# Attention scores on two 64-row halves of TensorE: three products per head, keys not doubled, queries not stacked

## The chip, the cores and the metric

The kernel runs on one core of one Trainium2 chip. The metric is the device time of one launch in microseconds (us). A core has five engines that work side by side and meet at semaphores: TensorE (matmuls; in the profile PE, its weight loads PEld), VectorE (DVE), ScalarE (ACT), GpSimd (POOL) and SyncE (SP, which here only issues DMA transfers). Matmul results go to PSUM, which is divided into banks; everything else lies in SBUF, with 128 partitions.

## What is computed

Block-causal attention, and a gated linear layer behind it:

```python
def _attn_ref(q, k, v):                       # each (8, 8, 576, 64)
    scores = np.matmul(q, k.transpose(0, 1, 3, 2)) / np.sqrt(64)
    mask = (pos[:, None] // 64) >= (pos[None, :] // 64)
    scores = np.where(mask, scores, -1e9)
    attn = softmax(scores)                    # max subtracted, + 1e-9 in the sum
    return np.matmul(attn, v)

def _moe_ref(x, w_gate, w_val, w_out):        # x is (4608, 512), d_ff 1536
    gate = 1 / (1 + np.exp(-(x @ w_gate)))
    return (gate * (x @ w_val)) @ w_out
```

The queries and keys are scaled by 5.7 and the gate's weights by 8, so the softmax and the gate are sharp. For this the kernel splits float32 operands into a high part H (float32r, which TensorE takes at its fast rate) and the rest L, and adds products of the parts. The three weights come as 64-bit floats and are converted on the chip.

## The kernel before

**Stages.** The 64 heads are worked on as 32 pairs of two heads (4 pairs per batch). One pair is one round of the loop `for p in range(n + 1)` (L753). In a round, the first half of pair p (`first`, L487: scores, exponentials) alternates with the second half of pair p-1 (`last`, L488: transposes of the probabilities, the product with V) and with `prep(p + 1)` (L244), which splits the next pair's keys and queries; the loads of pair p+2 are issued in between (L766 and L797). As soon as a batch of four pairs is done, a third of the first MLP layers (`mlp1`, L548, four of twelve blocks of d_ff) runs as filling: after each step of attention the loop takes some matmuls of it (L777 to L783). The weights of this filling are converted piece by piece during pairs 3 to 7 (`CONV_PLAN`, L25), mostly on VectorE. After the last pair comes the rest of the MLP (from L800), a seven-product scheme over two thirds of d_ff. It isn't touched, except that its buffers `raw` (L647) are named by tags of the first stage.

**The operands of the scores.** Queries and keys arrive by DMA in 32-wide blocks (L209 to L216) and are transposed on VectorE, so that the 64 features of head 0 lie in partitions 0 to 63 and those of head 1 in 64 to 127. A product of TensorE contracts over all 128 partitions, so each head is given all of them: `KD` holds, for each head, the high part of the keys twice, one copy in each half of the partitions, and likewise the rest; `QS` holds the high part of the scaled queries in one half and the rest in the other. One product with the high keys thus gives qH kH + qL kH, and a second with the rest of the keys adds qH kL + qL kL. To get there, prep casts the keys on ScalarE (L256), subtracts on VectorE (L257), and issues three copies from SBUF to SBUF for the keys (two at L260, one at L280) and four for the queries (L279), all on SP's queue. The queries are first split in place in the tiles `rk` and `rq` into which the loads of the pair after the next will go. Pair 0 has a path of its own with fewer steps (L262, L282).

**The scores.** `s_main(i)` (L330) does 128 query rows against the first 128 (i+1) keys, for i = 3, 2, 1, 0, so 512, 384, 256 or 128 columns. For i = 3 and 2 each head has its own PSUM bank, and one head's two products, the mask (a memset, L349), the maximum (a reduction, L350) and the exponential (L342) are issued before the other head's. For i = 1 and 0 both heads share one bank, one memset (L358) and one reduction (L359). `s_tail` (L365) does the last 64 query rows of both heads at once: `QS` is zero outside its own columns, so one product gives rows of head 0 and rows of head 1; that takes four products for each of two halves of the 576 keys.

**Order.** Each engine works through its own instructions in order. All matmuls of attention are recorded under the helper's line 225, all transposes under 228. The pool `ps_a` has six banks that are handed out in turn. The helper `behind` (L57) puts one instruction after another on the same engine without a semaphore; `mark("SP", ...)` in the loads (L214) makes the fetches of the MLP's weights (L77) queue behind them.

Of the kernel before, what the change touches and what calls it, by code (L numbers as in the profile page):

```python
# [29 lines left out]
def attn_glu_kernel(ctx: ExitStack, tc: tile.TileContext, q, k, v, w_gate, w_val, w_out, out):  # L30
    nc = tc.nc
# [117 lines left out]
    with ExitStack() as s2:  # L149
# [25 lines left out]

        QSs = [cv.tile([P, 2, 640], F32R, name=f"QS{i}") for i in range(2)]
        for QS in QSs:
            nc.gpsimd.memset(QS[:, 0, S:].bitcast(F32), 0.0)
            nc.gpsimd.memset(QS[:, 1, 0:64].bitcast(F32), 0.0)

# [4 lines left out]
        QM = (0, 128)  # L185
        QT = (512, 0)

        pairs = [(b, hp) for b in range(B) for hp in range(NP)]
        state = {}
# [7 lines left out]
        def load(p, what):  # L197
            b, hp = pairs[p]
            h0 = 2 * hp
            for name in what:  # L200
# [9 lines left out]
                for h in range(2):  # L210
                    parts = [(0, 0, S)] if name == "k" or h == 0 else [(64, 0, 512), (0, 512, 64)]
                    for j in range(2):
                        for c0, t0, n in parts:
                            mark("SP", nc.sync.dma_start(  # L214
                                out=r[64 * h + 32 * j:64 * h + 32 * j + 32, c0:c0 + n].rearrange("p (t a) -> p t a", a=32),
                                in_=src[b, h0 + h, t0:t0 + n, 32 * j:32 * j + 32].rearrange("(t p) a -> p t a", p=32)))  # L216
# [26 lines left out]

        def prep(p):  # L244


            KD = cv.tile([P, 2, 2, S], F32R, name="KD", bufs=2)
            QS = QSs[p % 2]
# [5 lines left out]
            if p:  # L254

                nc.scalar.copy(out=KD[:, 0, 0], in_=kT)  # L256
# [4 lines left out]
            else:  # L261
                for h in range(2):  # L262
                    s, o = halves(h)
                    nc.scalar.copy(out=KD[s, h, 0], in_=kT[s])
                    nc.vector.tensor_sub(out=KD[s, h, 1], in0=kT[s], in1=KD[s, h, 0].bitcast(F32))
                    nc.sync.dma_start(out=KD[o, h].bitcast(F32), in_=KD[s, h].bitcast(F32))
# [4 lines left out]
            if p:  # L271

                qH, qL = rk.bitcast(F32R), rq.bitcast(F32R)
                nc.scalar.mul(out=qH, in_=qT, mul=scale)
                nc.vector.scalar_tensor_tensor(out=qL, in0=qT, scalar=scale, in1=rk, op0=ALU.mult, op1=ALU.subtract)
                for e, src in enumerate((rk, rq)):
                    for h in range(2):
                        s, o = halves(h)
                        dma = nc.sync.dma_start(out=QS[o if e else s, h, 64 * h:64 * h + S].bitcast(F32), in_=src[s])  # L279
                behind(nc.sync.dma_start(out=B, in_=A).ins, dma.ins)  # L280
            else:
                for h in range(2):  # L282
                    s, o = halves(h)
                    c = slice(64 * h, 64 * h + S)
                    nc.scalar.mul(out=QS[s, h, c], in_=qT[s], mul=scale)
                    nc.vector.scalar_tensor_tensor(out=QS[o, h, c], in0=qT[s], scalar=scale,
                                                   in1=QS[s, h, c].bitcast(F32), op0=ALU.mult, op1=ALU.subtract)
# [4 lines left out]
            if whole(p):  # L292
                VS = at.tile([P, 5, 2 * D], F32, name="VS", bufs=2)
                nc.gpsimd.tensor_copy(out=VS, in_=rv)
                state[p] = KD, QS, VS
                return
# [11 lines left out]
            state[p] = KD, QS, (VS, V4)  # L308

        def attend(p):  # L310
            b, hp = pairs[p]
            KD, QS, VS = state.pop(p)
# [17 lines left out]
            def s_main(i):  # L330
# [5 lines left out]
                def scores(ps, h):  # L336
                    for e in range(2):
                        matmul(ps, lhsT=QS[:, h, QM[h] + i * P:QM[h] + (i + 1) * P], rhs=KD[:, h, e, :n],
                                         start=(e == 0), stop=(e == 1))

# [4 lines left out]
                if i >= 2:  # L345
                    for h in range(2):
                        ps = bank()[:, :n]
                        scores(ps, h)
                        nc.vector.memset(ps[0:64, n - 64:n], -1e9)  # L349
                        mark("DVE", nc.vector.tensor_reduce(out=nm[:, c0 + h:c0 + h + 1], in_=ps, axis=AX.X,  # L350
                                                            op=ALU.max, negate=True))
                        exps(ps, h)
                        yield
                else:
                    pv = bank()[:, :2 * n].rearrange("p (h n) -> p h n", h=2)
                    for h in range(2):
                        scores(pv[:, h], h)
# [3 lines left out]
                    for h in range(2):  # L361
                        exps(pv[:, h], h)
# [645 lines left out]
```

## Time and profile before

| what | value |
|---|---|
| median of 3 runs | 1294.96 us (1289.36 to 1296.46) |
| the profiled execution | 1295.23 us |
| its span, first to last instruction | 1293.1 us |
| mean granted clock of TensorE | 0.983 |
| instructions | 21797, of them 7312 matmuls |
| moved by DMA | 189.31 MB in 269359 packets |

In the profile's rows, `L225 PE MATMUL bank<-KD,QS 128*128 128x288 f32` means: line 225, engine PE, a matmul that reads the tiles KD and QS and writes a bank, on 128 rows and 128 columns of the array, with 128x288 elements streamed. Behind x stands the number of instructions, then the busy time in us and the mean duration of one in ns, then the idle time of the engine just before them and what ended it. A matmul's end is modelled and matmuls overlap, so the sum of their durations is more than the time they take. A row of the timeline gives the start, the length from the first start to the last end, and how many of a kind follow each other. A row of the chain gives a start, a length and what the end of the program waited for in that time. The row `PEclk` gives the clock granted to TensorE in tenths, in 40 slices of the span; 9 is 90% or more.

### The profile page before, as it was taken

What the parts mean: (1) busy time and instruction counts of PE and PEld (TensorE: products, weight loads), DVE (VectorE), ACT (ScalarE), POOL (GpSimd) and SP (SyncE); (2) the same over time, 40 slices, a digit from 0 to 9 for tenths busy, and PEclk for the clock granted to TensorE, in tenths of its full rate; (3) what the DMA queues carried; (4) which work ended last, traced back from release to release, by engine and by line L of the source; (5) the groups of instructions that cost most, each with busy time, mean ns of one, the idle gap of its engine ahead of it and who ended that gap; (6) DMA issues with size and microseconds to landing.
All of it is one profiled execution on the core that took longest, in us unless ns stands there. A gap on an engine that the chain in (4) does not pass through costs nothing.

```text
span 1293.1 us, 21797 instructions
## 1 busy us (share of the span) xinstructions
PE 1219.4 (94%) x7312; PEld 1129.5 (87%) x7312; DVE 996.0 (77%) x2153; ACT 736.8 (57%) x1829; POOL 390.0 (30%) x400
## 2 busy tenths in 40 slices
PE   4879899999999999999999899999999999999996
PEld 3769779999899998999989888999989989999995
DVE  6789988978889788887797897776679557656743
ACT  4767667877788787887754445344445424313411
POOL 1113223434344343443430013312321323542431
PEclk8989999999999999999999899999999999999999
DMA  7787676676766767668531424522538542552443
GB/s 146 159 199 187 161 143 151 127 178 125 157 144 129 176 127 155 155 127 189 128 108 56 166 82 159 187 80 109 187 139 297 195 154 69 170 180 67 144 148 97
DMA packets 269359, 189.31 MB, mean 146 GB/s; under 512 B 199808, under 2 KB 220288, under 8 KB 268608
## 3 DMA queue, kind: packets, MB, share of 16 engines
q1 hardware_dynamic: 259392, 169.04, 51.4%
q10 hardware_dynamic: 9856, 18.88, 4.1%
q8 instruction: 58, 0.95, 0.3%
q14 instruction: 53, 0.43, 0.1%
HBM read 94.37 MB, written 47.19 MB: 109 GB/s over the span
## 4 chain that ended last, share of the span: by engine, by line
PE 59%; DVE 17%; DMA 10%; ACT 5%; issue 4%; SPq 3%; POOL 1%; ACTq 0%; DVEq 0%; POOLq 0%
PE b L817 20%; PE bank L225 10%; PE m L875 8%; PE m L114 7%; PE m L123 5%; PE b L875 4%; PE bank L228 3%; DMA KD<-KD 2%; DMA pr<-part_d 2%; DVE P L397 2%; PE bank L114 2%; SPq L214 1%; DVE XL L716 1%; ACT P L342 1%; DVE KD L257 1%
## 5 line engine op out<-in xcount | busy, mean ns | idle before, releaser
L817 PE MATMUL b<-XH,w 128*128 128x384 f32 x1344 | 353.7, 338 | 9.7 <-ACT ost L576 3.1
L817 PEld LDWEIGHTS b<-XH,w 128*128 128x128 f32 x1344 | 246.0, 189 | 17.1 <-DVE v L853 5.1
L817 PE MATMUL b<-XL,w 128*128 128x384 f32 x672 | 225.7, 337 | 0.0
L225 PE MATMUL bank<-KD,QS 128*128 128x288 f32 (+4 forms) x768 | 162.2, 334 | 27.6 <-DMA KD<-KD 20.3
L225 PEld LDWEIGHTS bank<-KD,QS 128*128 128x128 f32 x768 | 118.7, 197 | 38.1 <-issue 18.9
L342 ACT ACTIVATE P<-bank,nm 128x512 f32<-128x512 f32 (+3 forms) x256 | 134.1, 529 | 29.2 <-DVE nm L359 16.3
L817 PEld LDWEIGHTS b<-XL,w 128*128 128x128 f32 x672 | 127.3, 190 | 1.3
L875 PE MATMUL m<-wo,hH 128*128 128x512 f32 x384 | 125.3, 392 | 0.3 <-ACT wo L684 0.3
L228 PE MATMUL bank<-ident,P 128*128 128x128 f32 x640 | 94.8, 280 | 15.7 <-DVE P L397 15.7
L114 PE MATMUL m<-XH,wv 128*128 128x288 f32 x448 | 105.0, 302 | 2.7 <-DVE h L135 1.4
L114 PE MATMUL m<-XH,wg 128*128 128x288 f32 x448 | 105.8, 303 | 0.2 <-ACT t L133 0.2
L890 POOL TENSOR_TENSOR pr<-pr,pr 128x512 f32<-128x512 f32 x36 | 48.0, 1333 | 167.4 <-DMA pr<-part_d 163.1
L228 PEld LDWEIGHTS bank<-ident,P 128*128 128x128 f32 x640 | 77.5, 144 | 22.8 <-issue 9.3
L225 PE MATMUL bank<-G1H,VS 128*128 128x320 f32 (+2 forms) x352 | 93.3, 346 | 0.9 <-ACT G1H L321 0.9
L397 DVE TENSOR_SCALAR P<-P,sm 128x512 f32<-128x512 f32 (+3 forms) x256 | 90.8, 412 | 1.2
L840 ACT ACTIVATE g<-g 128x384 f32<-128x384 f32 x72 | 37.0, 524 | 94.3 <-DVE g L853 64.5
L875 PEld LDWEIGHTS m<-wo,hH 128*128 128x128 f32 x384 | 72.0, 188 | 14.3 <-ACT wo L684 0.6
L715 ACT CAST XH<-XB 128x1536 fp32r<-128x1536 f32 (+2 forms) x72 | 65.8, 938 | 29.3 <-DVE XB L713 22.0
L323 DVE TENSOR_TENSOR G1L<-bank,G1H 128x512 fp32r<-128x512 f32 (+1 forms) x120 | 74.3, 626 | 10.5 <-ACT G1H L321 9.1
L321 ACT CAST G1H<-bank 128x512 fp32r<-128x512 f32 (+1 forms) x120 | 63.6, 545 | 31.3 <-PE bank L228 27.8
L114 PEld LDWEIGHTS m<-XH,wv 128*128 128x128 f32 x448 | 76.2, 189 | 3.4 <-DVE h L135 1.9
L716 DVE TENSOR_TENSOR XL<-XB,XH 128x1536 fp32r<-128x1536 f32 (+2 forms) x72 | 77.3, 1081 | 1.5 <-ACT XH L715 1.5
(178 smaller groups left out, 2936.2 us busy)
## 6 DMA issues: line engine op xcount, KB each, us to landing
KD<-KD SPq DMA_DIRECT2D x95, 288.0 KB, 3.9
pr<-part_d SPq DMA_DIRECT2D x72, 256.0 KB, 3.6
QS<-rqk SPq DMA_DIRECT2D x124, 144.0 KB, 3.1
rqk<-in_k_dram SPq DMA_DIRECT2D x128, 72.0 KB, 3.3
xT_d<-xT ACTq DMA_DIRECT2D x32, 288.0 KB, 3.1
XB<-xT_d SPq DMA_DIRECT2D x16, 576.0 KB, 5.7
part_d<-ost SPq DMA_DIRECT2D x36, 256.0 KB, 3.9
out_dram<-ost SPq DMA_DIRECT2D x36, 256.0 KB, 2.8
```

What stands on the lines that cost most here:

```text
L114: mm = nc.tensor.matmul(ps, lhsT=lh, rhs=rh, start=(i == 0), stop=(i == n - 1))
L123: mm = nc.tensor.matmul(ps, lhsT=lh[:, f, t * P:(t + 1) * P], rhs=rh, start=(i == 0), stop=(i == n - 1))
L225: pe_last[:] = [nc.tensor.matmul(*args, **kw).ins]
L228: pe_last[:] = [nc.tensor.transpose(*args).ins]
L321: mark("ACT", nc.scalar.copy(out=dst[0], in_=src))
L323: mark("DVE", nc.vector.tensor_sub(out=dst[1], in0=src, in1=dst[0].bitcast(F32)))
L342: mark("ACT", nc.scalar.activation(out=Pi[:, h], in_=ps, func=AF.Exp, bias=nm[:, c0 + h:c0 + h + 1], accum_out=sm[:, c0 + h:c0 + h + 1]))
L397: mark("DVE", nc.vector.tensor_scalar_mul(Pi[:, h], Pi[:, h], sm[:, c0 + h:c0 + h + 1]))
L715: nc.scalar.copy(out=XO[j][0][:, a:b], in_=x)
L716: sub = nc.vector.tensor_sub(out=XO[j][1][:, a:b], in0=x, in1=XO[j][0][:, a:b].bitcast(F32))
L817: mm = nc.tensor.matmul(ps, lhsT=lh, rhs=rh, start=(first and k == 0), stop=(k == n - 1), skip_group_check=not first)
L875: mm = nc.tensor.matmul(po[t], lhsT=lh[:, f, t * P:(t + 1) * P], rhs=rh, start=(half == 0 and i == 0), stop=(half == 1 and i == 5))
```

## The change

The two heads' operands stay where the transposes leave them: `KQ` holds kH, kL, qH and qL, head 0 in partitions 0 to 63, head 1 in 64 to 127. Each score product works on 64 rows of the array, `tile_position=(64 * h, 0)`, and there are three per head, qH kH + qH kL + qL kH; the product of the two rests is left out. The products of the two heads alternate and write two banks. At all four widths each head now has its own bank, memset and reduction. The tail still uses all 128 rows: two small copies on GpSimd put the last 64 queries of each head into `QB`, which is zero elsewhere, and three products do both heads. The seven copies inside SBUF are gone, the load of the queries has four issues instead of six, pair 0 takes the same path as the others, the loads no longer mark SP's queue, and the buffers `raw` have tags of their own.

```diff
-        QSs = [cv.tile([P, 2, 640], F32R, name=f"QS{i}") for i in range(2)]
...
+        QBs = [at.tile([P, 2, 2, D], F32R, name=f"QB{i}") for i in range(2)]
+        for QB in QBs:
+            nc.gpsimd.memset(QB.bitcast(F32), 0.0)
...
+        PARTS = ((2, 0), (2, 1), (3, 0))
...
-                    parts = [(0, 0, S)] if name == "k" or h == 0 else [(64, 0, 512), (0, 512, 64)]
                     for j in range(2):
-                        for c0, t0, n in parts:
-                            mark("SP", nc.sync.dma_start(
...
+                        nc.sync.dma_start(
+                            out=r[64 * h + 32 * j:64 * h + 32 * j + 32].rearrange("p (t a) -> p t a", a=32),
+                            in_=src[b, h0 + h, :, 32 * j:32 * j + 32].rearrange("(t p) a -> p t a", p=32))
...
+            KQ = cv.tile([P, 4, S], F32R, name="KQ", tag="KD", bufs=2)
...
-                nc.scalar.copy(out=KD[:, 0, 0], in_=kT)
-                nc.vector.tensor_sub(out=KD[:, 0, 1], in0=kT, in1=KD[:, 0, 0].bitcast(F32))
-                A, B = (KD[s, 0].bitcast(F32) for s in (slice(0, 64), slice(64, 128)))
-                for dst in (KD[0:64, 1], KD[64:128, 1]):
-                    nc.sync.dma_start(out=dst.bitcast(F32), in_=B)
...
+            nc.scalar.copy(out=KQ[:, 0], in_=kT)
+            nc.vector.tensor_sub(out=KQ[:, 1], in0=kT, in1=KQ[:, 0].bitcast(F32))
...
-                        dma = nc.sync.dma_start(out=QS[o if e else s, h, 64 * h:64 * h + S].bitcast(F32), in_=src[s])
-                behind(nc.sync.dma_start(out=B, in_=A).ins, dma.ins)
...
+            nc.scalar.mul(out=KQ[:, 2], in_=qT, mul=scale)
+            nc.vector.scalar_tensor_tensor(out=KQ[:, 3], in0=qT, scalar=scale, in1=KQ[:, 2].bitcast(F32),
+                                           op0=ALU.mult, op1=ALU.subtract)
+            for h in range(2):
+                nc.gpsimd.tensor_copy(out=QB[rows(h), :, h], in_=KQ[rows(h), 2:4, S - D:].bitcast(F32))
...
+                pss = [bank()[:, :n] for _ in range(2)]
+                for j, (a, b_) in enumerate(PARTS):
                     for h in range(2):
...
+                        matmul(pss[h], lhsT=KQ[rows(h), a, i * P:(i + 1) * P], rhs=KQ[rows(h), b_, :n],
+                               start=(j == 0), stop=(j == 2), tile_position=(64 * h, 0))
+                for h, ps in enumerate(pss):
+                    nc.vector.memset(ps[0:64, n - 64:n], -1e9)
+                    mark("DVE", nc.vector.tensor_reduce(out=nm[:, c0 + h:c0 + h + 1], in_=ps, axis=AX.X,
+                                                        op=ALU.max, negate=True))
+                    exps(ps, h)
...
-                    for h in range(2):
-                        for e in range(2):
-                            matmul(ps, lhsT=QS[:, h, QT[h]:QT[h] + P], rhs=KD[:, h, e, 288 * half:288 * half + 288],
...
+                    for j, (a, b_) in enumerate(PARTS):
+                        matmul(ps, lhsT=QB[:, a - 2].rearrange("p h q -> p (h q)"),
+                               rhs=KQ[:, b_, 288 * half:288 * half + 288], start=(j == 0), stop=(j == 2))
...
-            return (cv.tile([P, 4 * P, 2], U32, name="raw", tag=f"QS{i}"),
+            return (cv.tile([P, 4 * P, 2], U32, name="raw", tag=f"raw{i}"),
```

More of the change, by code (lines that the diff above doesn't have):

```diff
@@ L343, in exps @@
                                                      accum_out=sm[:, c0 + h:c0 + h + 1]))
[L345 removed]
+                pss = [bank()[:, :n] for _ in range(2)]
+                for j, (a, b_) in enumerate(PARTS):
                     for h in range(2):
[L347 to L352, printed above, removed]
[L353 to L363 removed]
+                        matmul(pss[h], lhsT=KQ[rows(h), a, i * P:(i + 1) * P], rhs=KQ[rows(h), b_, :n],
[5 more added lines that the diff above has]
+                    exps(ps, h)
+                    if i >= 2 or h:
+                        yield
             def s_tail():
```

50 lines of the change are left out of this document (6 added, 44 removed).

## Prediction

> **What bounds the kernel now.** I read four views in this order: the page, the table of stretches, the timeline of TensorE, and the chain of waits. On the page three rows matter: the share of each engine, the granted clock in 40 slices, and the group of all score products.
>
> ```profile
> PE 1219.4 (94%) x7312; PEld 1129.5 (87%) x7312; DVE 996.0 (77%) x2153; ACT 736.8 (57%) x1829; POOL 390.0 (30%) x400
> PEclk8989999999999999999999899999999999999999
> L225 PE MATMUL bank<-KD,QS 128*128 128x288 f32 (+4 forms) x768 | 162.2, 334 | 27.6 <-DMA KD<-KD 20.3
> ```
>
> A share of the whole span says little, so I cut the span at the first score product of pairs 1, 4, 9 and 31, at the end of the first GLU part and at the end. Columns: us, busy time (and instructions) of PE, PEld, DVE, ACT and POOL, clock, DMA share, GB/s.
>
> ```profile
> 0.00:27.05 27.05, 8.69 (x33) 7.50 (x33) 15.70 (x34) 11.98 (x29) 3.44 (x14) 0.88 0.78 150
> 27.05:78.06 51.01, 41.81 (x227) 35.43 (x228) 38.62 (x108) 35.10 (x101) 4.25 (x4) 0.90 0.81 173
> 78.06:188.21 110.15, 97.75 (x598) 86.81 (x597) 101.20 (x246) 77.49 (x216) 28.21 (x25) 0.95 0.74 170
> 188.21:635.16 446.95, 434.89 (x3059) 410.24 (x3058) 381.53 (x929) 350.27 (x998) 169.95 (x196) 1.00 0.68 148
> 720.00:1293.10 573.10, 552.88 (x2862) 512.06 (x2860) 391.51 (x682) 218.85 (x381) 164.71 (x144) 0.99 0.43 143
> ```
>
> There are two regimes. From 188 to 635 us, pairs 9 to 30 (22 pairs), TensorE is busy 434.89 of 446.95 us at the full clock of 1.00: a microsecond of matmul more or less per pair is one on the clock. Before 188 us, pairs 0 to 8, it isn't: in pairs 1 to 3 no engine is busy throughout and the DMA share is 0.81; in pairs 4 to 8 VectorE is busy 101.20 of 110.15 us. After 635 us nothing is changed but the names of two buffers; it only moves.
>
> **What a score product costs.** Matmuls overlap in the trace, so the mean duration isn't the price; the distance between two starts is. A run of n of one shape lasts one duration and n-1 distances.
>
> ```profile
> 508.54 0.62 PE L123 MATMUL m<-wo,hH 128*128 128x512 f32 x2
> 509.00 0.39 PE L123 MATMUL m<-wo,hL 128*128 128x512 f32 x1
> ...
> 1000.63 0.51 PE L817 MATMUL b<-XH,w 128*128 128x384 f32 x2
> ...
> 1000.98 0.33 PE L817 MATMUL b<-XL,w 128*128 128x384 f32 x1
> ```
> ```profile
> 299.80 0.56 PE L225 MATMUL bank<-KD,QS 128*128 128x288 f32 x3
> 300.20 0.29 PE L114 MATMUL m<-XH,wv 128*128 128x288 f32 x1
> ...
> 305.06 0.67 PE L225 MATMUL bank<-KD,QS 128*128 128x256 f32 x4
> ```
> ```profile
> 510.46 0.64 PE L225 MATMUL bank<-KD,QS 128*128 128x128 f32 x4
> ```
> ```profile
> L225 PE MATMUL bank<-KD,QS 128*128 128x256 f32 x88 | 14.1, 283 | 0.0
> L225 PE MATMUL bank<-KD,QS 128*128 128x128 f32 x88 | 13.8, 279 | 0.0
> ```
>
> So 512 columns cost 0.62-0.39 = 0.23 us, 384 cost 0.51-0.33 = 0.18, 288 cost (0.56-0.29)/2 = 0.13, 256 cost (0.67-0.28)/3 = 0.13, 128 cost (0.64-0.28)/3 = 0.12. The last two hardly differ, because the weight load sets the distance there:
>
> ```profile
> 510.44 0.53 PEld L225 LDWEIGHTS bank<-KD,QS 128*128 128x128 f32 x4
> 510.88 0.19 PEld L123 LDWEIGHTS m<-wo,hH 128*128 128x128 f32 x1
> ```
>
> (0.53-0.19)/3 = 0.113 us per load. Now a pair (the 88 products of 256 columns in these 447 us are 4 in each of 22 pairs). Before, the main score tiles issue two products for each of two heads at 512, 384, 256 and 128 columns: 4 x (0.23+0.18+0.13+0.12) = 4 x 0.66 = 2.64 us. After, there are three products per head, each on half of the rows. Every matmul of this trace uses 128 rows, so no row shows whether two halves work at once. The ends are: one after another, 6 x 0.66 = 3.96 us (+1.32); both streams and loads in parallel, 3 x 0.66 = 1.98 (-0.66). Between them, streams in parallel but loads one at a time, as in every row above: a step of two heads then takes 0.23 at 512 and 2 x 0.113 = 0.226 at the other widths, 3 x (0.23+0.678) = 2.72 (+0.08). The tail stays on all 128 rows and goes from 8 to 6 products of 288: 2 x 0.13 = -0.26. Net per pair and over 22 pairs: +1.06 (+23), -0.92 (-20), -0.18 (-4). I take the middle one, -4: the loads in the rows come singly, and the two heads have different rows and different banks, so nothing else that the code shows ties their streams together. The Trainium skill, TensorE: Matmul & The Clock Gate, Part 3, says that matmuls in distinct row groups run concurrently, and gives 3.07x for four; by it alone the term would be -20, and no run here shows it yet.
>
> **What changing the layout costs.** The four main tiles lie between work on the full array (the MLP products, transposes and the tail), so the array goes from whole to halves and back 4 times a pair: 8 changes, 176 in 22 pairs. No row shows one. The lower end is 0: matmuls of unlike kinds follow without a gap in the rows above. The upper end is a restart: the matmuls already running finish, and the next load has nothing to hide under. A wait of TensorE shows this:
>
> ```profile
> 302.62 0.41 PE L225 MATMUL bank<-G1L,VS 128*128 128x320 f32 x1
> 302.87 0.31 PE L225 MATMUL bank<-G1H,VS 128*128 128x320 f32 x1
> 303.02 0.31 PE L225 MATMUL bank<-G1L,VS 128*128 128x320 f32 x1
> ```
>
> The uncovered load adds 0.41-0.31 = 0.10; a matmul lasts 0.31-0.15 = 0.16 beyond the distance to the next start (303.02-302.87 = 0.15). So at most 0.26. I take 0.15, a little over the middle and nearer to the restart, because by those rows a product is still under way for 0.16 us when the next could start, and it would have to be out of the way: 176 x 0.15 = +26. The Trainium skill, TensorEngine Tiling (Array Packing), Key Properties, states that switching the mode drains TensorE; it gives no price, and speaks against this change.
>
> **What the transfers were worth.** Gone are 3 copies of keys and 4 of queries per pair; loads of q and k go from 10 to 8 issues.
>
> ```profile
> KD<-KD SPq DMA_DIRECT2D x95, 288.0 KB, 3.9
> ...
> QS<-rqk SPq DMA_DIRECT2D x124, 144.0 KB, 3.1
> ```
> ```profile
> 7.83 3.36 DMA KD<-KD
> ...
> 11.33 1.20 PE bank L225 x2
> ...
> 18.59 4.25 DMA KD<-KD
> ...
> 22.92 3.88 DMA KD<-KD
> ...
> 27.05 2.04 PE bank L225 x4
> ```
> ```profile
> L269 DVE STREAM_TRANSPOSE rvT<-rqk 128x576 f32<-128x576 f32 x32 | 24.5, 767 | 0.2
> L274 ACT ACTIVATE rqk<-rvT 128x576 fp32r<-128x576 f32 x31 | 21.3, 688 | 13.1 <-DVE rvT L269 8.9 <-DVE nm L381 3.9
> L275 DVE SCALAR_TENSOR_TENSOR rqk<-rvT,rqk 128x576 fp32r<-128x576 f32 x31 | 27.1, 874 | 3.9 <-ACT rqk L274 3.8
> ```
>
> - Pair 0: its first product waits until 11.33 us for a copy. Without it the way is transpose, cast and rest of q from 7.2 us on, 0.77+0.69+0.87 = 2.3, so 9.5 at the latest: about -2.
> - Pair 1: two copies end the wait at 27.05. Without them those 2.3 us start at about 18.6, so 21: -6 at most. Pair 0's own second half then fills some of it; I take -4.
> - Pairs 1 to 3: 51.0 us with VectorE busy 38.6, so -12 at most. The copies and the loads behind them share SP's queue; the loads of pair p+2 no longer wait for copies that read rq and rk. I take -4.
> - Pairs 4 to 8: VectorE has 9.0 us free, less what is added to it. Added are, per pair, two reductions' fixed part and two memsets net.
>
> ```profile
> L350 DVE TENSOR_REDUCE nm<-bank 128x1 f32<-128x512 f32 x64 | 43.2, 681 | 0.5
> L377 DVE TENSOR_REDUCE nm<-bank 128x1 f32<-128x288 f32 x64 | 27.4, 440 | 3.9 <-PE bank L225 3.5
> L349 DVE MEMSET bank<- 64x64 f32 x128 | 14.0, 112 | 28.9 <-PE bank L225 27.4 <-ACT KD L256 0.6
> L358 DVE MEMSET bank<- 64x128 f32 x64 | 10.6, 165 | 5.3 <-PE bank L225 3.9
> ```
>
>   681 and 440 ns over 224 columns give 1.08 ns a column and 0.13 us fixed; 2 x 0.13 + 4 x 0.112 - 2 x 0.165 = +0.38 us a pair, +2 in five pairs. Freed: late weight and key copies, as the one of 5.61 us below, -5 of the 9. Net -3.
> - Pairs 9 to 30: TensorE waited for these copies 2.4 us in all: -1. VectorE's 0.38 us hides there (381.53 of 446.95 busy); if TensorE had no work left, it would cost 8.
>
> ```profile
> 160.14 5.61 DMA KD<-KD
> ```
> ```profile
> PE bank L225 <- DMA KD<-KD: 2.4, 2, 1.4
> ```
>
> Together -14; between -5 (only pairs 0 and 1, partly) and -25 (every bound reached). The two small copies per pair on POOL are on no path: POOL is busy 169.95 of 446.95, and the next pair's tail, which reads them, comes a pair later. They are queued ahead of the copy of V, which waits for TensorE anyway; without that cover each would cost about its own duration, some 0.3 us by the copy of 64x128:
>
> ```profile
> L306 POOL COPY V<-rvT 64x128 f32<-64x128 f32 x24 | 8.1, 337 | 49.1 <-DMA rvT<-in_v_dram 24.5 <-PE bank L225 8.6 <-PE m L114 7.9
> ```
>
> Dropping mark("SP") from the loads lets weight fetches pass them in SP's queue; I cost that at nothing beyond the above, since those weights are used a pair later. A score bank's first reduction now waits for five products instead of two, and two banks are held at once, not one, at 256 and 128 columns; with six banks and other matmuls between, I cost it at 0, at most about 0.5 us a pair (three products more).
>
> **The sum.** The profiled execution took 1295.2 us (1293.1 of span and 2.1 around it), 0.3 over the median of the three runs shown. 1295.2 - 14 (transfers) - 4 (products) + 26 (changes of layout) = 1303.2; I say 1303. About 0.5%, 6.5 us, is what a measurement of this kernel can tell from no change, so this stands just beyond it.
>
> **Rivals.**
> 1. Free changes. Halves and whole array follow each other as unlike matmuls do now, with no gap. Then 1295 - 14 - 4 = 1277, and with parallel loads 1261; say 1270. For it: the copies vanish, and no row has a gap between unlike matmuls. Against it: all of those use the same 128 rows. It decides once a change costs under some 0.06 us (176 x 0.06 = 11).
> 2. Full drain: at every change TensorE finishes all that runs and loads uncovered, 176 x 0.26 = +46, 1295 - 14 - 4 + 46 = 1323. For it: the restart at 302.62 shows what that costs. Against: in all other rows a load runs beside the matmul before it, and may do so across a change too. The rule in the Trainium skill, TensorEngine Tiling (Array Packing), Key Properties, would mean this case if nothing of it is hidden.
> 3. No parallel streams. The heads' products run one after another: 1295 - 14 + 23 = 1304 with free changes, 1330 with 0.15 each; say 1320. For it: every row shows one stream at a time. Against: the heads share neither rows nor banks.
> 4. The transfers were hidden anyway: pairs 1 to 8 are held by VectorE and the chain of softmax, and only pair 0 and part of pair 1 gain. -14 shrinks to -5, the rest as forecast: 1312. For it: VectorE's 101.20 of 110.15 us. Against: the copies end the waits of pairs 0, 1 and 8 in the chain.
>
> **How the numbers follow.** Forecast 0.32 (own range 1275 to 1313: a change at 0.05 to 0.2, loads parallel or single), free changes 0.29, full drain 0.17, no parallel streams 0.16, hidden transfers 0.06. Faster, under 1288.7: 0.27 of rival 1 and 0.12 of the forecast, 0.39. Within 0.5%: 0.02 of rival 1, 0.08 of the forecast, 0.02 of rival 3, 0.01 of rival 4, 0.13. Slower, over 1301.7: 0.12 of the forecast, 0.17, 0.14 and 0.05 of rivals 2, 3 and 4, 0.48. Single cases of the forecast lie on both sides, so the sign is nearly open. The range from 1267 to 1335 leaves out about 0.07 below (rival 1 with parallel loads) and 0.12 above (rivals 2 and 3 with both dear changes and one stream).
>
> **What would show each step.** Parallel streams: in the new profile two score products of 512 columns, one per head, start within a few hundredths of a microsecond of each other, and a block of six spans about 3 x 0.23 plus one duration, not 6 x 0.23. Loads: starts 0.11 us apart at 128 and 256 columns if they come singly. Layout changes: a gap before the first and after the last product of each block of six, in PEld, which no semaphore ends; 0.15 is forecast, 0 is rival 1, 0.26 is rival 2. Transfers: the first product before 10 us, pair 1 near 21 us, pair 9 near 174 instead of 188. I am wrong if the block of six has no gap at its ends, if the heads don't overlap, or if pair 9 doesn't start earlier.

## The result and the profile after

The kernel after took 1335.95 us, median of four runs (1333.62 to 1339.28), against 1295.28 of the kernel before in four runs beside it: ratio 1.0325, interval 1.0286 to 1.0364. That is 33 us above the forecast of 1303, and 1 us above the top of its range. The profiled execution took 1333.62 us, with a span of 1331.8.

Rows of the profile of after, as shown for before: engines, clock, and the score products, which here stand in two rows (the main tiles, and the tail).

```profile
PE 1281.2 (96%) x7504; PEld 1132.0 (85%) x7504; DVE 998.1 (75%) x2279; ACT 736.6 (55%) x1827; POOL 408.7 (31%) x462
PEclk9999999999999999999999999999999999999999
L220 PE MATMUL bank<-KQ 64*128 64x512 f32 (+3 forms) x768 | 145.0, 358 | 9.0 <-ACT KQ L257 9.0
L220 PE MATMUL bank<-KQ,QB 128*128 128x288 f32 x192 | 36.6, 318 | 1.6 <-ACT P L311 1.5
```

The idle time ahead of the score products fell from 27.6 to 10.6 us, the granted clock is 0.9 or more in every slice (0.992 on average, 0.983 before), and yet TensorE is busy 61.8 us longer. The stretches of after, cut as before at the first score product of pairs 1, 4, 9 and 31 and at the end of the first GLU part:

```profile
0.00:21.39 21.39, 8.48 (x38) 6.88 (x40) 13.08 (x32) 9.75 (x23) 4.43 (x16) 1.00 0.80 199
21.39:73.98 52.59, 45.93 (x247) 33.95 (x247) 41.04 (x124) 36.22 (x105) 7.10 (x10) 0.94 0.50 97
73.98:182.72 108.74, 101.35 (x632) 82.42 (x632) 104.92 (x272) 78.53 (x220) 30.97 (x35) 1.00 0.39 89
182.72:668.82 486.10, 486.10 (x3184) 419.39 (x3183) 379.35 (x1006) 348.42 (x988) 184.33 (x239) 1.00 0.30 68
668.82:758.60 89.78, 86.29 (x545) 79.05 (x545) 69.59 (x167) 46.14 (x113) 15.60 (x18) 0.98 0.31 101
758.60:1331.80 573.20, 553.02 (x2866) 510.29 (x2864) 390.07 (x682) 217.54 (x380) 166.25 (x144) 0.99 0.42 143
```

The stretch from pair 31 to the end of the first GLU part was in before:

```profile
635.16:720.00 84.84, 83.35 (x542) 77.50 (x543) 67.40 (x155) 43.06 (x106) 19.46 (x18) 1.00 0.35 112
```

Pair 9 starts 5.5 us earlier (182.72 against 188.21). Then pairs 9 to 30, the late stretch from here on, take 486.10 us instead of 446.95: +39.15, nearly the whole loss. Pair 31 with the end of the first GLU part takes 4.9 us more (89.78 against 84.84); some 1.4 us of that are six MLP products of 512 columns that ran ahead of the cut in before and run behind it in after. The last stretch is the same. In the late stretch TensorE is busy every microsecond, where before it was idle for 12 (434.89 of 446.95). So the copies' waits are gone, and the time has gone into the products or between them. Two places of the timeline of after show where; first a tile of 384 columns, engine PE and then PEld:

```profile
320.01 0.43 PE L114 MATMUL m<-XH,wv 128*128 128x288 f32 x2
320.37 0.79 PE L220 MATMUL bank<-KQ 64*128 64x384 f32 x3
321.09 0.50 PE L220 MATMUL bank<-G,VS 128*128 128x256 f32 x2
```
```profile
320.37 0.47 PEld L220 LDWEIGHTS bank<-KQ 64*128 64x128 f32 x3 [0.16 <-issue]
321.08 0.41 PEld L220 LDWEIGHTS bank<-G,VS 128*128 128x128 f32 x3 [0.25 <-ACT P L311]
```

Only three of the six products stand here; the other head's three come later, after other work. **In:** two products of 288 columns start at 320.01, 0.13 apart, so the next could start at 320.27 and starts at 320.37: a gap of 0.10. Its weights are loaded at the same moment, 320.37, not under the product before: three products 0.18 apart and one duration of 0.33 make 0.69, and the row says 0.79, so 0.10 is the uncovered load. **Out:** three distances of 0.18 end at 320.91, plus that 0.10 is 321.01; the next product starts at 321.09, 0.08 later, with its load at 321.08, uncovered again (0.50 for two of 256 columns instead of 0.28+0.13 = 0.41). So at this tile a change of layout costs a gap of 0.08 to 0.10 and a load of about 0.10: 0.17 to 0.20 us, each way.

Then a tile of 512 columns whose six products stand together:

```profile
337.94 0.28 PE L220 MATMUL bank<-G,VS 128*128 128x256 f32 x1
338.15 0.98 PE L220 MATMUL bank<-KQ 64*128 64x512 f32 x6
339.06 0.45 PE L220 MATMUL bank<-G,VS 128*128 128x256 f32 x2
```

Six products take 0.98 us, as long as three would by the distances: 2 x 0.23 + 0.39 + 0.10 of load = 0.95, while six one after another would take 1.64. The heads run side by side, if they stand together. Counted through the trace of after, they mostly don't: of 197 blocks of half-array products 136 hold three, which I take for those of one head (the rows name no head), and 55 hold six. The order in which TensorE gets its instructions is fixed when the kernel is built. I take it that it goes by when banks are expected to come free: a tile's two banks come free at different times, so three products of one head are put in, then other work, then the other three. e5 and e15 below fit this: with both banks claimed first and the order forced, the six stay together. In the late stretch there are 146 blocks instead of the 88 that I had assumed (4 tiles in 22 pairs): 292 changes instead of 176.

The trace shows the same picture at every one of these changes, in and out: the first load begins together with its product (within 3 ns), 0.07 us before the modelled end of the product ahead. Between whole-array products the next one starts 0.16 us before that end (median), so each change leaves a gap of 0.09 us. Measured block by block (up to the second product behind it, less the usual distances), the median extra is 0.31 us at 128 columns, 0.35 at 256 and 0.37 at 384: 0.16 to 0.19 per change, about 0.17 over all of them.

### The profile page after: what moved, and what is told of

Read it like the earlier page. It is cut to its first block, busy times and chain, and to the rows that moved or that the text cites. A ratio compares the mean times of both kernels' runs of the same rounds, so it can differ in the third digit from the quotient of the medians.

```text
span 1331.8 us, 21723 instructions
## 1 busy us (share of the span) xinstructions
PE 1281.2 (96%) x7504; PEld 1132.0 (85%) x7504; DVE 998.1 (75%) x2279; ACT 736.6 (55%) x1827; POOL 408.7 (31%) x462
## 4 chain that ended last, share of the span: by engine, by line
PE 76%; DVE 10%; DMA 5%; POOL 3%; issue 2%; ACT 2%; SPq 1%; POOLq 0%; ACTq 0%; DVEq 0%
PE bank L220 19%; PE b L777 17%; PE m L114 14%; PE m L835 8%; PE m L123 7%; PE bank L223 6%; PE b L835 4%; DMA pr<-part_d 3%; DVE XL L676 2%; PE bank L114 1%; POOL pr L850 1%; DMA XB<-xT_d 1%; DVE nm L322 1%; POOL hL L785 1%; DMA rqk<-in_k_dram 1%
## 5 line engine op out<-in xcount | busy, mean ns | idle before, releaser
L220 PE MATMUL bank<-KQ 64*128 64x512 f32 (+3 forms) x768 | 145.0, 358 | 9.0 <-ACT KQ L257 9.0
L220 PEld LDWEIGHTS bank<-KQ 64*128 64x128 f32 x768 | 91.1, 191 | 45.7 <-issue 20.1
L322 DVE TENSOR_REDUCE nm<-bank 128x1 f32<-128x512 f32 (+3 forms) x256 | 120.2, 480 | 3.2
L114 PE MATMUL m<-XH,wg 128*128 128x288 f32 x448 | 110.1, 310 | 0.0
L114 PE MATMUL m<-XH,wv 128*128 128x288 f32 x448 | 109.5, 308 | 0.0
L223 PEld LDWEIGHTS bank<-ident,P 128*128 128x128 f32 x640 | 74.7, 142 | 17.9 <-ACT P L311 7.1
L141 POOL TENSOR_TENSOR hL<-h,hH 128x288 fp32r<-128x288 f32 (+1 forms) x56 | 48.3, 862 | 103.1 <-ACT hH L140 85.5
```

Of the source, the lines that this page charges most:

```text
L114: mm = nc.tensor.matmul(ps, lhsT=lh, rhs=rh, start=(i == 0), stop=(i == n - 1))
L220: pe_last[:] = [nc.tensor.matmul(*args, **kw).ins]
L223: pe_last[:] = [nc.tensor.transpose(*args).ins]
```

## The experiments

**Theory:** the loss is the number of blocks of half-array products, two changes of 0.19 us each, and what a split block loses in side-by-side running. **Rivals:** products on half the rows are slow in themselves or never run side by side; or the waits moved to something else.

**e1_together and e2_together_serial.** One tile of two banks for both heads, so that both come free at once; in e2 also the order is forced, head 0's three products first.

```diff
+ pair = ps_a.tile([P, 2, 512], F32, name="pair", bufs=1)
- pss = [bank()[:, :n] for _ in range(2)]
+ pss = [pair[:, h, :n] for h in range(2)]
```

> Changed kernel, but the two heads' main scores lie in one PSUM tile of two banks (one such tile, four single banks left), so that all six products of a tile become ready at once and stay together: 246 changes of layout instead of 394, and the heads' streams always side by side. Theory (a change of layout costs about 0.19 us, and splitting the six also puts the heads one after another): -28 for the changes, about -24 for the streams, some 15 given back as waits of TensorE, 1299 (1290 to 1310). Rival 1 (half-array products are simply more products, the order doesn't matter): 1330 or more. Rival 2 (holding two banks per tile is what hurts): no faster than 1336, since here they are held even more strictly.

> As the run before, but within the six the three products of head 0 come first and then the three of head 1, in a fixed order: the same number of layout changes, the same banks, but no streams side by side except at the seam. Theory: about 1.9 us more per pair, 22 to 32 pairs bound by TensorE, less some waits: 1335 (1325 to 1345). Rival (the nearly equal starts in the trace are only records, the array works through them one after another): equal to the run before within 5 us.

Measured: 1456.38 us (ratio 1.1265, 1.1224 to 1.1306) and 1466.25 (1.1338, 1.1301 to 1.1376). Both missed. The waits of e1 from 200 to 700 us (total, times, longest) and its products:

```profile
PE pair L220 <- ACT P L311: 45.6, 39, 5.3
```
```profile
400.93 0.79 PE L220 MATMUL pair<-KQ 64*128 64x384 f32 x6 [1.00 <-ACT P L311]
404.89 0.62 PE L220 MATMUL pair<-KQ 64*128 64x256 f32 x6 [1.25 <-ACT P L311]
411.53 0.55 PE L220 MATMUL pair<-KQ 64*128 64x128 f32 x6 [0.45 <-ACT P L311]
```

There is one such tile, and each tile of scores waits until ScalarE has read the last; the granted clock of the profiled execution is 0.946, against 0.992 of after. What the runs do show is in the last rows: six products of 128 columns in 0.55 us. One duration is 0.27, so five steps take 0.28; with one load at a time, five steps of 0.113 would take 0.57. The weight loads of the two heads run side by side too. And e2's blocks are no longer than e1's:

```profile
402.77 0.80 PE L220 MATMUL pair<-KQ 64*128 64x384 f32 x6 [1.00 <-ACT P L311]
406.74 0.63 PE L220 MATMUL pair<-KQ 64*128 64x256 f32 x6 [1.25 <-ACT P L311]
413.38 0.56 PE L220 MATMUL pair<-KQ 64*128 64x128 f32 x6 [0.44 <-ACT P L311]
```

though head 1's three come behind head 0's three. The starts in e2's blocks still come in twos, 0.01 us apart. The record names no head, but in the blocks of three of after no two starts are closer than 0.11 us, so I read each two as one of each head: within a block, the order doesn't matter. Why e2 takes 10 us more than e1 stays open.

**e3_full_array.** No change of layout at all: all products on the whole array, so that both heads are summed. All else of the change stays.

```diff
- matmul(pss[h], lhsT=KQ[rows(h), a, i * P:(i + 1) * P], rhs=KQ[rows(h), b_, :n], ..., tile_position=(64 * h, 0))
+ matmul(pss[h], lhsT=KQ[:, a, i * P:(i + 1) * P], rhs=KQ[:, b_, :n], ...)
```

> Changed kernel, but each main score product uses all 128 rows without a tile position, so that it sums the scores of both heads (that part of the result is changed); same number of products, same loads, banks, VectorE and ScalarE work, no copies, no change of layout. Theory: all 394 changes at 0.19 go, -75; the products always one after another, +22; waits come back, +15: 1298 (1288 to 1310). Rival 1 (three products instead of two are the cost): 1336 or more, since nothing runs side by side any more. Rival 3 (the lost copies and the new order of loads cost): 1336.

Measured: 1298.87 (ratio 1.0056, 1.0038 to 1.0074). The half-array layout as built costs 37 us, although here all six products of a tile run one after another. Its pairs 1 to 3 and its late stretch:

```profile
23.10:69.74 46.64, 41.51 (x247) 34.99 (x247) 40.59 (x123) 35.85 (x105) 7.16 (x10) 0.99 0.51 107
179.10:633.10 454.00, 452.22 (x3186) 430.09 (x3185) 384.99 (x1007) 346.28 (x989) 183.69 (x239) 1.00 0.32 73
```

**e4_three_blocks.** As e1, and the 256- and 128-column tiles' twelve products in one block.

> As the first run of this set, but the products of the two narrow tiles (256 and 128 columns) are issued together into one pair of banks: 184 changes of layout instead of 246. Theory: 62 x 0.19 = -12 against the first run, about 1287 (1278 to 1297). Rival (the price is not per change): equal to the first run, or slower since the softmax of the narrowest tile starts earlier than it is needed.

Measured: 1408.31 (1.0901, 1.0869 to 1.0934), a miss. It is 48 us less than e1, but the wait for the one two-bank tile hides any count.

**e5_claimed.** Banks as in after, but a 64-column whole-array product writes into the second bank first, and the six follow it in order.

```diff
+ if (j, h) == (0, 0):
+     matmul(pss[1][:, :64], lhsT=KQ[:, 2, :P], rhs=KQ[:, 0, :64], start=True, stop=True)
+ before = pe_last[0]
  matmul(pss[h], ...)
+ behind(pe_last[0], before)
```

> Changed kernel with six single banks again, but ahead of the six products of each main tile stands a product of 64 columns on the full array into the second head's bank (overwritten by that head's first product), and the seven are chained in order. So the six only start when both banks are free, and stay together, without the two-bank tile that made TensorE wait in the first set. 256 changes of layout instead of 394. Theory (0.19 us per change, streams side by side when together): -26 for the changes, -24 for the streams, +10 for the 128 extra products of about 0.11 us as far as TensorE is the bound, 0 to +15 of waits that come back: 1303 (1294 to 1313). Rival (the number of half-array products or the two banks per narrow tile are the cost): 1336 or more.

Measured: 1302.84 (1.0088, 1.0068 to 1.0108), 93 blocks in the late stretch. Keeping the six together takes 33 us off after's time.

**e6_wide_halves and e7_split_halves.** As e3, but one tile on halves: that of 512 columns, whose six mostly stand together, or that of 384, which is mostly split.

```diff
+ HALVES = (3,)        # e7: (2,)
+ r = rows(h) if i in HALVES else slice(0, P)
```

> Full-array kernel of the first set (each product sums both heads' scores, that part of the result is changed), but the tile of 512 columns alone is done on halves, with the tile position. In the order of the program 29 of its 32 sixes stay together. Theory, against the full-array kernel's 1299: streams side by side save 3 x 0.23 = 0.68 us a pair, two changes cost 0.38: about -0.3 in each of 22 pairs, 1292 (1287 to 1297). Rival (any use of halves costs more than it saves): slower than 1301.

> The same full-array kernel, but the tile of 384 columns alone is done on halves; here the program's order puts other work between the two heads' products in nearly all pairs. Theory: nothing runs side by side, four changes a pair at 0.19: +0.76 in each of 22 pairs, 1315 (1307 to 1322). Rival (the cost is that of half-array products as such, the same for both widths): the same as with the 512-column tile on halves, within 5 us.

Measured: 1290.82 (0.9991, 0.9977 to 1.0006) and 1314.71 (1.018, 1.016 to 1.02), so 8 us below and 16 above e3. The late stretches of e6 and e7, beside 454.0 of e3:

```profile
179.18:629.85 450.67, 448.87 (x3184) 419.03 (x3183) 384.21 (x1006) 347.35 (x989) 181.14 (x239) 1.00 0.33 73
181.38:649.13 467.75, 467.50 (x3186) 428.02 (x3184) 382.70 (x1007) 347.62 (x989) 183.37 (x239) 1.00 0.31 71
```

There e6 gains 3.3 us and e7 loses 13.8; the rest of e6's 8 us lies from pair 31 on, and no run explains it. The same layout gains on one tile and loses on another. The widths differ too, but by the distances 384 columns kept together would also save more (3 x 0.18 us) than two changes cost; so the difference is whether the heads stand together. e7 has 45 blocks with nothing side by side: 13.8 us are 0.15 per change.

**e8_no_copies.** The kernel before without its seven copies from pair 2 on.

```diff
- for dst in (KD[0:64, 1], KD[64:128, 1]):
+ for dst in (KD[0:64, 1], KD[64:128, 1]) if p < 2 else ():
# the four query copies and the last key copy likewise; KD in two fixed tiles
```

> The kernel before without the seven copies inside SBUF from pair 2 on: the key and query halves that they fill keep the values of pairs 0 and 1 (that part of the result is left out); all matmuls, VectorE and ScalarE work and loads stay. It measures what the transfers cost outside the first two pairs. Theory: nearly hidden, since TensorE waited for them only 2.4 us in pairs 9 to 30 and VectorE bounds pairs 4 to 8: -3, 1288 (1284 to 1291). Rival (as the prediction had it, -8 without the first two pairs): 1283 or less.

Measured: 1272.20 (0.9857, 0.9837 to 0.9877), a miss. The copies are worth 19 us by the medians (23 by the two profiled executions), and in the late stretch, where I had put 1, they are worth 16:

```profile
182.56:613.50 430.94, 429.24 (x3053) 408.56 (x3052) 384.01 (x921) 348.46 (x987) 170.53 (x195) 1.00 0.34 77
```

430.94 against 446.95. Of the 16 us, 10.4 are idle time of TensorE (12.06 against 1.70), 1.4 are the six MLP products that here too fall behind the cut, and for the other 4 I have no row. e8 takes the copies' traffic away with their waits (DMA share 0.34 against 0.68); the trace of before shows the waits, under other names. By shape, the late stretch of before has

```profile
L225 PE MATMUL bank<-KD,QS 128*128 128x512 f32 x88 | 25.1, 407 | 8.0 <-DMA KD<-KD 2.4 <-DVE h L135 1.7 <-DVE sm L390 1.7
```

8.0 us of idle ahead of the pair's first tile, and I took only the 2.4 that name the copy. But follow one pair, SP's queue and then TensorE, in the timeline of before:

```profile
300.84 1.11 SPq L260 DMA_DIRECT2D KD<-KD  x2
302.04 2.31 SPq L203 DMA_DIRECT2D rvT<-in_v_dram  x2
304.40 0.65 SPq L205 DMA_DIRECT2D rvT<-in_v_dram  x1
305.14 2.47 SPq L279 DMA_DIRECT2D QS<-rqk  x4
307.67 0.59 SPq L280 DMA_DIRECT2D KD<-KD  x1
```
```profile
312.39 1.18 PE L225 MATMUL bank<-KD,QS 128*128 128x512 f32 x4 [0.85 <-DVE sm L390]
```

The last copy is issued from 307.67 to 308.26 and lands at 312.26 by the trace's record of landings; the product starts at 312.39. The row names VectorE's `sm`, which a product of scores doesn't read. Pair by pair, the 8.0 us of idle stand in 13 of the 22 pairs, and in each of the 13 the last key copy lands 0.09 to 0.25 us ahead of that product.

**e9_copy_earlier and e10_copy_on_act.** The kernel before, with its last key copy ahead of the last two query copies, or on ScalarE's queue.

```diff
- behind(nc.sync.dma_start(out=B, in_=A).ins, dma.ins)
# e9:
+ if (e, h) == (0, 1):
+     copy = nc.sync.dma_start(out=B, in_=A)
...
# e10:
+ nc.scalar.dma_start(out=B, in_=A)
```

> The kernel before, complete, with one thing moved: the last of the three key copies is issued between the second and the third of the four query copies instead of behind the fourth. Same instructions, same traffic. Theory (the 16 us that the late pairs lose to the copies are waits of each pair's first score product for the last copy, whatever engine the profile names): the last copy is issued about 1.2 us earlier, the last query copy 0.6 later but it lands faster; the wait of 0.57 us a pair nearly goes: 1281 (1277 to 1287). Rival (it is the traffic of the copies, or the engines that the rows name): 1291, no change.

> The kernel before, complete, with the last key copy issued from ScalarE's queue, without an order against the query copies. Theory: it can start as soon as the first two copies have landed, about 1.5 us earlier, and SP has one issue less: 1281 (1276 to 1288), less if the wait holds up ScalarE's own work behind it. Rival (traffic): 1291.

Measured: 1291.30 (0.999, 0.9974 to 1.0006) and 1308.50 (1.0119, 1.0093 to 1.0145). Both missed. In e9 the idle time by shape becomes

```profile
L225 PE MATMUL bank<-KD,QS 128*128 128x512 f32 x88 | 27.2, 413 | 3.7 <-DMA QS<-rqk 2.9 <-DVE G L327 0.2
```

It is 3.7 instead of 8.0, most of it now ended by the query copies that were put behind, and the late stretch is nearly as long as ever (446.0 us): part of the wait went to the next copy, and TensorE waits elsewhere for the rest. In e10 the late stretch and the same row are

```profile
187.82:645.43 457.61, 438.98 (x3060) 411.35 (x3058) 385.20 (x926) 349.23 (x990) 171.94 (x195) 1.00 0.67 144
L225 PE MATMUL bank<-KD,QS 128*128 128x512 f32 x89 | 25.8, 406 | 1.9 <-DVE nm L350 1.2 <-DVE G L323 0.6
```

The wait ahead of the first tile is down to 1.9 us, but TensorE is idle for 18.6 us in all, instead of 12. The copy now stands in ScalarE's queue among its own work; that it holds that work up is only argued. Of the three things tried on the copies, only taking them away gains.

**e11_claimed_low and e12_claimed_two.** As e5, with one block for the tiles of 256 and 128 columns, and in e12 also one for those of 512 and 384, over four banks.

> The kernel with the claimed second bank, with the products of the 256- and the 128-column tile issued together into the same two banks: about 192 changes of layout instead of 256 and 32 small products less. Theory, against 1303: 62 x 0.19 = -12, small products -3: 1289 (1283 to 1296). Rival (count isn't the price): 1300 or more.

> As the run before, and the tiles of 512 and 384 columns also together, in four banks: about 128 changes of layout, two blocks a pair. By the count alone 1303 - 24 = 1279. But four of six banks are held by one block, as the two-bank tile held its two, and waits of TensorE for the exponentials come with it: I expect 1290 (1278 to 1310).

Measured: 1307.17 (1.0099, 1.0073 to 1.0126) and 1319.04 (1.0189, 1.0162 to 1.0217). Both missed: 101 and 66 blocks in the whole kernel instead of e5's 133, and no gain (e11's interval overlaps e5's, e12 is slower). Three waits of TensorE that are 1.0, 0.3 and 1.0 us in e5's late stretch are in e11's, whose profiled execution was its slowest (1314.47 us),

```profile
PE bank L220 <- ACT G L295: 9.0, 11, 2.0
PE bank L220 <- ACT P L313: 4.6, 8, 1.6
PE bank L220 <- DVE G1L L297: 2.9, 5, 0.8
```

I read this so: a longer block gives softmax and the product with V their scores later, and other work fewer banks meanwhile. For e12 I have no such clear row: TensorE is idle for 15.3 us of its late stretch, against 3.9 in e5. That it is the four banks is only argued.

**e13_extra_full and e14_extra_half.** The price of a change by itself: e3 with six more 64-column products a pair, on the whole array or on 64 rows.

```diff
+ matmul(pss[0][:, :64], lhsT=KQ[:, 2, :P], rhs=KQ[:, 0, :64], start=True, stop=True)
# e14:
+ matmul(pss[0][:, :64], lhsT=KQ[rows(0), 2, :P], rhs=KQ[rows(0), 0, :64], start=True, stop=True, tile_position=(0, 0))
```

> The kernel after with whole-array score products (both heads summed, as in e3_full_array), and 190 further whole-array products of 64 columns, six a pair: one before each main tile's first product and one before each half of the tail. Their results are overwritten. It is the control for e14_extra_half. From pair 9 on each costs a load distance, 0.11 to 0.13 us, 132 of them +16; before that about +3. Expected 1298.9 + 19 = 1318, range 1312 to 1324.

> The same 190 further products, but each on 64 rows: nothing else differs from e13_extra_full, so the difference is the price of two changes of layout per extra product by itself. My theory from the after trace (0.09 us of gap and 0.10 us of uncovered load, each way): the 132 products from pair 9 to 30 cost 264 x 0.195 = 51 us and the earlier ones, which partly hide, some 10: 1318 + 61 = 1379, range 1368 to 1392. Rival, by the difference of e7 and e3 in the same pairs (13.8 us over 88 changes, 0.157): 264 x 0.157 = 41 and 8, 1367. The prediction's 0.15 says the same as the rival. If a change cost nothing, 1318.

Measured: 1307.28 (1.0118, 1.0095 to 1.0141) and 1356.04 (1.0492, 1.047 to 1.0513). Both lie below their ranges. Their difference, 49 us, is what the rival expected (41 and 8, at 0.157 per change) and the forecast's 0.15 with it; my theory of 0.195 expected 61. The late stretches of e13 and e14, beside the 454.00 of e3:

```profile
178.69:645.69 467.00, 465.99 (x3317) 444.55 (x3316) 390.96 (x1006) 347.71 (x988) 179.70 (x239) 1.00 0.32 71
```
```profile
188.28:693.05 504.77, 504.77 (x3316) 456.15 (x3315) 388.66 (x1012) 349.93 (x989) 181.10 (x239) 1.00 0.29 66
```

132 blocks of one product each: e14 less e13 is 37.8 us, 0.143 per change. But e14 less e3 is 50.8, 0.385 per block or 0.19 per change. The two agree if a small product on the whole array costs 0.10 (13.0 / 132, e13 less e3), and on halves nothing beyond its two changes. The timeline of e14 fits that:

```profile
313.48 0.29 PE L114 MATMUL m<-XH,wg 128*128 128x288 f32 x1
313.71 0.29 PE L220 MATMUL bank<-KQ 64*128 64x64 f32 x1
313.93 0.67 PE L220 MATMUL bank<-KQ,QB 128*128 128x288 f32 x3
```

0.23 us from the 288-column product to the small one, where 0.13 is usual (+0.10), and 0.22 from the small one to the next, where e13 has 0.03 to 0.11. So the price is 0.19 with the small product in it, and 0.14 beyond what that product would cost anyway. With e7's 0.15 and the trace of after, a change costs 0.14 to 0.19 us; my theory's 0.195 is the upper end.

**e15_claim_dve.** The kernel after, complete, its six kept together by a column that VectorE writes into both banks.

```diff
+ claim = nc.vector.memset(pss[h][:, :1], 0.0).ins    # h = 0, then 1 behind it
- for h in range(2):
+ for h in (1, 0):     # each product behind the last
```

> The complete kernel after, with the six products of a tile kept together without the 64-column products of e5: VectorE writes one column of zeros into both banks of a tile, the second bank behind the first, and the products begin with the second head's, so that they start when both banks are free; each is put behind the last. 124 blocks of six. My theory (blocks cost by their number, and e5 lost time only to its 64-column products, 88 with 11.6 us from pair 9 to 30, some 4 us elsewhere): 1302.8 - 15 = 1288, range 1282 to 1297. Rival: a claim that waits for a bank holds up VectorE's queue behind it and the products then wait for VectorE instead, 1303 to 1320.

Measured: 1295.29 (1.0022, 1.0009 to 1.0035), inside the range of my theory but 7 us above its value: about 40 us faster than after, and still no faster than before. Its late stretch, with exactly 88 blocks, and two waits:

```profile
179.90:635.71 455.81, 445.32 (x3191) 394.09 (x3190) 386.93 (x1188) 351.95 (x994) 186.75 (x241) 1.00 0.33 73
```
```profile
PE bank L223 <- DVE bank L319: 2.6, 3, 1.0
PE bank L220 <- DVE bank L319: 2.4, 5, 0.7
```

TensorE is idle for 10 us again, half of it behind the claim (line 319). Of all complete kernels tried here none beats the one before by more than its interval.

## Why the prediction was wrong

The sign with the largest chance was right, the time 33 us too low. By the profiled executions 18 us of this miss lie in the late stretch, 7.5 before pair 9 and 5 from pair 31 on. By the steps:

- **What bounds the kernel:** right for the late stretch, which TensorE bounds and which holds nearly all of the loss. "After 635 us nothing is changed but the names of two buffers" is wrong: pair 31 does its scores there, and the stretch takes 4.9 us more.
- **Number of changes: this step failed.** That "the array goes from whole to halves and back 4 times a pair: 8 changes, 176 in 22 pairs" was read off the code's loop. The program has 292, because most tiles' six products are split in two. e15, with 88 blocks and so the 176 changes of the forecast, takes 1295, e5 with nearly so many 1303.
- **Price of a change:** 0.15 forecast, 0.14 to 0.19 found (e14 less e13, e7 less e3, e14 less e3), so about right. The rest of the bound of 0.26 wasn't paid: of the 0.16 by which a product outlasts the next start, 0.09 is left as a gap. The Trainium skill, TensorEngine Tiling (Array Packing), Key Properties, states that switching the mode drains TensorE. The trace agrees as far as it goes, with a gap and an uncovered load at each change; the product behind starts 0.07 us before the modelled end of the one ahead, so whether the array is quite empty by then it doesn't show.
- **Products: this step failed too.** -4 was forecast, which is -6 for the tail and +2 for the main tiles. I took streams in parallel and loads one at a time. With the heads together both are parallel (0.55 us for six of 128 columns), which was the end at -20. The Trainium skill, TensorE: Matmul & The Clock Gate, Part 3, says that matmuls in distinct row groups run concurrently; that row agrees. With the heads split nothing is parallel: by the forecast's distances and a count of which heads overlap in the trace, the main tiles' products of after take 11 us more than those of before.
- **Transfers, pairs 9 to 30: failed as well, on the other side.** -1 forecast, 16 by e8. The row that named a copy for 2.4 us was taken for all of the copies' waits; the others bore the names of engines whose results the product doesn't read, while the last key copy landed just ahead of it.
- **Transfers before pair 9:** -13 forecast, -5.5 found. Pair 0 starts its products at 9.04 (9.5 at the latest was forecast) and pair 1 at 21.39 (21). Pairs 4 to 8 take 108.74 us, hardly less than the 110.15 of before, and 109.39 in e3 and 109.98 in e8: held without the copies too, as rival 4 had it, where I had put -3. Pairs 1 to 3 show another loss. Without copies they take 45.54 us in e8 and 46.64 in e3, so the forecast's -4 of 51.01 was there to be had; but after, which differs from e3 in the layout alone, takes 52.59. The forecast put the layout at nothing there. How much is the layout itself and how much the lower clock (0.94 against 0.99) no run separates.

In the late stretch: 292 x 0.17 = +50, products +11, tail -6, waits -16, together +39, as measured (+39.15). With 0.19 per change it would be 5 us more. The same distances and waits, with no change of layout and all six products one after another (+29), give 454 for e3, as measured (454.00). The forecast had +26, -4 and -1, +21. The two sides partly cancel, and that was luck: changes and products came out 33 us dearer than forecast there, and the copies' absence 15 us more useful. Of the rivals, 3 at its upper end (1330) and 2 (1323) came nearest, each with part of the mechanism: the heads run one after another only where they are split, and the price of a full drain, 0.26, was too high and its count too low.

How much of the split's loss is changes and how much serial products isn't separated by a run. The 58 extra blocks are 16 to 22 us at 0.14 to 0.19 per change; after less e15 is 30 in the late stretch, with 10 us of idle in e15 that after doesn't have.

## What to carry to other kernels

Count what a layout change costs in the order in which instructions reach the engine, not in the loop that writes them: two results that come free at different times pull a block apart, and each part pays 0.3 to 0.4 us here. Keep the parts together only by what holds no bank and no queue longer, or the saving is spent on waits (e1, e4, e11). And where a wait bears the name of an engine whose result the waiting product doesn't read, look for the transfer that lands at that moment, and price it by taking the transfer away (16 us in the late stretch here, against 2.4 in the row).

## What the runs showed of the hardware

- A change between whole array and 64-row halves costs 0.14 to 0.19 us in each direction (e14 less e13, e14 less e3). At every change of after's late stretch the load and the product behind begin together, 0.07 us before the modelled end of the product ahead, where 0.16 is usual.
- Two halves load weights and stream at the same time: six products of 128 columns in 0.55 us, steps of about 0.11 for two heads.
- Products on the second half seem to start beside those on the first although three products of the first stand ahead of them in the order (e2: 0.80 against e1's 0.79 us at 384 columns; which head a start belongs to is inferred).
